# A cached-attention and gated-MLP decode kernel: the first load of each of two queues is issued as two transfers, 16 partitions and then 112

## The chip, the cores and the metric

The kernel runs on one core of a Trainium2 chip. The metric is the device time of one execution in microseconds (us), median of several runs. The core has a matrix engine (PE, TensorE), a vector engine (DVE, VectorE), a scalar engine (ACT), GpSimd (POOL) and SyncE (SP). Data come from the device memory into SBUF, an on-chip memory of 128 partitions, by 16 transfer engines (DMA). In this kernel SP and ACT issue the transfers, each into a queue of its own; the profile calls SP's queue q1 and ACT's q10.

## The reference: what is computed

One token `x` of width 448 goes through two branches, and a gate mixes them.

```python
g = _sigmoid((x * gate_w).sum(-1, keepdims=True))
# A: 16 query heads, 8 K/V heads, 65536 cached positions, head size 256
q = (x @ wq)
scores = einsum("bhqd,bhkd->bhqk", q, k) * (Dh ** -0.5)
a = (softmax(scores) @ v) @ wo
# B: inner width 1792
gate, up = x @ W_gate, x @ W_up
b = (gate * (gate > 0) * up) @ W_down
return g * a + (1 - g) * b
```

The K and V caches are 8 x 65536 x 256 in bf16 each, 268 MB each. All weights together are about 12 MB.

## The kernel before

Every operation and every transfer gets an engine and a key, an intended time. `_Plan` sorts each engine's list by key and puts in the semaphore waits. So the order on each queue is the order of the keys.

K and V come in tiles of 8.39 MB (128 partitions of 65,536 B) into three buffers, `ring0` to `ring2`; a head has four tiles of each. VectorE transposes a K tile in place (L379), PE multiplies it with the spread-out query `xm` (L394, L420), and a row maximum and an exponential follow (L594 to L598). After a head's four K tiles its V tiles are multiplied with the weights. SP issues all the tiles, and waits before each until the buffer is free.

Before the first K tile come the small loads. The plan gives them these places:

- ACT's queue, in this order: the first 384 rows of `W_gate` (L254, semaphore `wf0`, into `wf3[0]`, a part of `ring2`), then `x` (L256), then `gate_w` (L257).
- SP's queue, in this order: the first 384 rows of `wq` (L525, semaphore `wq`, into `wq3`, a part of `ring2`), `W_up` (L540), the last 64 rows of `wq` (L526, into `ring1`), the first K tile (L587, into `ring0`), the last 64 rows of `W_gate` and `W_up` in small pieces (L405, after a memset by POOL), and, once the query's last product is there, `W_down` (L574) and the next K tiles.

For both first loads three rows of the matrix lie side by side in one partition, so a partition takes 3 x 1792 x 2 = 10,752 B of `W_gate` and 3 x 4096 x 2 = 24,576 B of `wq`.

What uses them: `x` starts the chain on VectorE (L310 to L322) that spreads it over partitions; then PE makes the query with `wq` (L345, waits for semaphore `wq`; L352) and the MLP's products with `W_gate` and `W_up` (L550, waits for `wf0`). The first transpose of a K tile comes after them.

The output is 448 values, stored by one transfer (L698) that the program waits for (L706).

Of the kernel before, what the change touches and what calls it, by code (L numbers as in the profile page):

```python
# [24 lines left out]
class _Plan:  # L25
# [13 lines left out]
    def dma(self, eng, key, sem, fn, deps=()):  # L39
        if sem not in self.dsem:  # L40
            self.dsem[sem] = self.es.enter_context(self.nc.semaphore("d_" + sem))
        o = _Op(eng, key, fn, deps, dma=sem)
        self.ops.append(o)
        return o
# [59 lines left out]
def bass_gated_mix__gqa_block_cached__glu_gated_reglu__decode_kernel(  # L104
# [24 lines left out]
    R3 = D // 128  # L129
    NR3 = R3 * 128  # L130
# [13 lines left out]
    with es:  # L144
# [42 lines left out]
        wq3 = ring[2][:, 0:R3 * NQ]  # L187
        wqa = ring[1][:, 0:NQ // 2]
        WB = R3 * NQ
        wf3 = [ring[2][:, WB + i * R3 * F:WB + (i + 1) * R3 * F] for i in range(2)]  # L190
# [18 lines left out]
        op, dma = pl.op, pl.dma  # L209
# [25 lines left out]
        t = 3.0  # L235
# [10 lines left out]
        for kind, i, _ in order:  # L246
# [4 lines left out]
        wo_sb = ring[slot["wo", 0]][:, 0:H * 4 * D].rearrange("p (h s n) -> p h s n", h=H, s=4)  # L251


        d_wg = dma("ac", -10, "wf0", lambda e: e.dma_start(  # L254
            wf3[0], B_W_gate[0:NR3, :].rearrange("(p k) f -> p (k f)", k=R3)))
        d_x = dma("ac", -9, "x", lambda e: e.dma_start(x_row, A_x[0, :, :]))  # L256
        d_gw = dma("ac", -8, "gw", lambda e: e.dma_start(gw_row, gate_w.rearrange("(o d) -> o d", o=1)))  # L257

# [151 lines left out]
        l_, qk, smax, aexp, pv, last = {}, {}, {}, {}, {}, {}  # L410
        pending = []

        def free(key):
            out_ = []
            for f in freed[key]:
                out_.append(l_[f] if isinstance(f, str) else qk[f[1]] if f[0] == "k" else pv[f[1]])
            return out_
# [104 lines left out]

        for kind, i, t in issue:
            if kind == "wq":
                l_["wq"] = dma("sp", t, "wq", lambda e: e.dma_start(wq3, A_wq[0:NR3, :].rearrange("(p k) n -> p (k n)", k=R3)))  # L525
                l_["wqh"] = dma("sp", t + 0.01, "wqh", lambda e: e.dma_start(  # L526
                    wqa, A_wq[NR3:D, :].rearrange("r (c n) -> (r c) n", c=2)))
                tq = tL["wq", 0]
# [9 lines left out]
            elif kind == "gu":  # L538
                t = tL["gu", 0]
# [43 lines left out]
            elif kind == "k":  # L583
                n = i
# [45 lines left out]
            elif kind in ("v", "vp"):  # L630
                if kind == "v":
                    n, lo, hi = i, 0, U
# [12 lines left out]
            elif kind == "wo":  # L645
# [6 lines left out]
                for k, (h0, h1, lo, hi) in enumerate(runs):  # L652
# [3 lines left out]
                    else:  # L656
                        o = wo_sb[:, h0, lo:hi, :]
                        v = A_wo[h0 * 512:h1 * 512, :].rearrange("(p s) n -> p s n", s=4)[:, lo:hi, :]
                    d_ = dma("sp", t + 0.01 * k, "wo%d%d" % (i, k), lambda e, o=o, v=v: e.dma_start(o, v),
                             free(("wo", 0)) if i == 0 else [])  # L660
# [19 lines left out]
        for i in range(len(WOP)):  # L680
            for k, (h, lo, hi) in enumerate(WOP[i]):
                key = tL["wo", i] + 0.01 * k
                if i == 1:
                    key = t7 + (-0.3 if h < NP else 0.6) + 0.01 * k
# [52 lines left out]
```

## Time and profile before

| | us |
|---|---|
| median of 3 runs | 1277.21 (1277.18 to 1277.37) |
| the profiled execution | 1277.21 |
| its span, first to last instruction | 1275.9 |
| VectorE busy | 683.4 (54%) |
| PE busy | 353.7 (28%) |
| ScalarE busy | 56.1 (4%) |
| moved from memory | 549.03 MB |

The span is what the trace covers; 1.31 us of the execution lie around it. The profile's page gives for 40 equal slices of the span the share of time in which each engine was busy and the GB/s that the transfers moved. A group's row gives source line, engine, operation and tiles, then busy time, the mean of one in ns, and the idle time of the engine in front of it with what ended it. The row of an issue gives the size and the time from issue to landing. In the table by stretches each line has the stretch, its length, the busy time of PE, of PE's weight loads, of VectorE, ScalarE and GpSimd, the granted clock of PE, the share of the transfer engines and GB/s. Packets are booked with their bytes where they end, so short stretches swing.

### The profile page before, as it was taken

The page shows a single profiled execution, that of the slowest core. Times are in us where ns is not written, and L with a number is a line of the kernel's source. Part 1 is how long each engine was busy: PE and PEld are TensorE (multiplying, and loading weights), DVE is VectorE, ACT ScalarE, POOL GpSimd, SP SyncE. Part 2 cuts the span into 40 slices and gives each one's busy share as a digit, 9 for nine tenths or more (in the row PEclk, how much of TensorE's full clock was granted, in tenths as well). Part 3 has the DMA queues.
Part 4 walks back from the last instruction along what each step waited for, and adds up shares of the span by engine and source line. Part 5 has one row for each costly group of instructions (what it writes and reads, how often), then busy time and mean ns, then how long its engine had stood idle before and what let it go on. Part 6 is the DMA issues. An engine that isn't in the chain of part 4 may idle for free.

```text
span 1275.9 us, 6860 instructions
## 1 busy us (share of the span) xinstructions
PE 353.7 (28%) x4446; PEld 71.6 (6%) x1875; DVE 683.4 (54%) x271; ACT 56.1 (4%) x104; POOL 10.6 (1%) x23
## 2 busy tenths in 40 slices
PE   3312323313122240133220242211323203322135
PEld 2000000000000000000000000000000000000010
DVE  2688733566534755445555454556535566336521
ACT  0000000000000000000000000000000000000000
POOL 3000000000000000000000000000000000000000
PEclk9566666665666565666755666656666556666577
DMA  9999999999999999999999999999999999999998
GB/s 407 433 436 434 438 428 429 442 427 436 431 426 448 429 428 434 430 434 438 428 434 438 430 434 428 432 438 438 428 428 436 436 438 428 428 438 436 434 417 372
DMA packets 11178, 549.46 MB, mean 431 GB/s; under 512 B 1255, under 2 KB 1386, under 8 KB 2154
## 3 DMA queue, kind: packets, MB, share of 16 engines
q1 hardware_dynamic: 11002, 547.66, 99.3%
q10 hardware_dynamic: 148, 1.38, 0.3%
q8 instruction: 24, 0.39, 0.1%
q14 instruction: 4, 0.03, 0.0%
HBM read 549.03 MB, written 0.00 MB: 430 GB/s over the span
## 4 chain that ended last, share of the span: by engine, by line
DVE 40%; DMA 28%; PE 17%; another core or an unknown queue 12%; ACT 1%; issue 1%; SPq 0%; ACTq 0%; DVEq 0%
DVE ring L379 32%; DMA ring<-in_A_k_cache_dram 24%; PE ST L394 5%; PE ST L420 5%; PE O L420 4%; DMA ring<-in_A_wo_dram 3%; DVE o_sb L429 2%; PE O L488 2%; DVE P L617 1%; DVE P L615 1%; ACT P L598 1%; DMA P<-in_A_x_dram 1%; DVE nmb L596 1%; DVE ST L594 1%
## 5 line engine op out<-in xcount | busy, mean ns | idle before, releaser
L379 DVE STREAM_TRANSPOSE ring<-ring 128x16384 uint32<-128x16384 uint32 (+1 forms) x36 | 552.3, 15345 | 315.9 <-DMA ring<-in_A_k_cache_dram 311.5
L394 PE MATMUL ST<-ring,xm 128*16 128x512 bf16 x1024 | 139.7, 537 | 769.2 <-DVE ring L379 769.2
L420 PE MATMUL ST<-ring,xm 128*16 128x512 bf16 x1024 | 136.7, 526 | 0.0
L420 PE MATMUL O<-ring,P 128*32 128x512 bf16 x1524 | 119.3, 425 | 0.0
L594 DVE COPY_PREDICATED ST<-bm,ST 128x512 f32<-128x512 uint16 x32 | 22.2, 693 | 169.3 <-PE ST L420 169.3
L598 ACT ACTIVATE P<-ST,nmb 128x512 bf16<-128x512 f32 x32 | 45.3, 1415 | 1099.3 <-DVE nmb L596 1099.3
L394 PEld LDWEIGHTS ST<-ring,xm 128*16 128x16 bf16 x1024 | 31.8, 115 | 925.8 <-DVE ring L379 797.9
L488 PE MATMUL O<-ring,P 128*32 128x512 bf16 (+1 forms) x524 | 56.7, 430 | 21.9 <-DMA ring<-in_A_v_cache_dram 21.9
L429 DVE CAST_PREDICATED o_sb<-bm,O 128x512 bf16<-128x512 uint16 (+1 forms) x33 | 22.3, 679 | 62.0 <-PE O L420 58.9
L615 DVE TENSOR_TENSOR P<-P,hs 128x2048 bf16<-128x2048 bf16 x8 | 18.3, 2292 | 8.7 <-ACT hs L612 8.7
L596 DVE TENSOR_REDUCE nmb<-ST 128x1 f32<-128x512 f32 x32 | 22.1, 691 | 1.1
L488 PEld LDWEIGHTS O<-ring,P 128*32 128x32 bf16 (+1 forms) x524 | 15.8, 114 | 119.3 <-issue 92.0
L617 DVE STREAM_TRANSPOSE P<-P 128x2048 bf16<-128x2048 bf16 x8 | 18.5, 2312 | 0.3
L622 PE MATMUL M_ps<-hs,ones_f 128*128 128x2 f32 x16 | 4.7, 363 | 46.0 <-DVE hs L621 46.0
L457 PE MATMUL M_ps<-emat,o_sb 128*64 128x2 bf16 x48 | 3.0, 184 | 22.1 <-ACT o_sb L439 22.1
L598 ACT ACTIVATION_READ_ACCUMULATOR P<-ST,nmb 128x1 f32 x32 | 8.5, 266 | 0.0
L345 PE MATMUL M_ps<-ring,P 128*128 128x256 bf16 x48 | 7.4, 330 | 0.3 <-DVE gb L297 0.3
L310 DVE COPY xm<-P 1x64 bf16<-1x64 bf16 x2 | 0.3, 189 | 11.9 <-DMA P<-in_A_x_dram 11.9
L622 PEld LDWEIGHTS M_ps<-hs,ones_f 128*128 128x128 f32 x16 | 4.0, 311 | 46.7 <-DVE hs L621 46.7
L608 PE MATMUL M_ps<-identf,hs 128*2 128x128 f32 x8 | 2.2, 277 | 15.7 <-DVE hs L606 15.7
L259 POOL MEMSET ring<- 64x7168 bf16 x1 | 6.1, 6064 | 0.3 <-POOLq L722 0.3
L345 PEld LDWEIGHTS M_ps<-ring,P 128*128 128x128 bf16 x48 | 5.6, 118 | 2.0 <-issue 0.4
(96 smaller groups left out, 82.6 us busy)
## 6 DMA issues: line engine op xcount, KB each, us to landing
ring<-in_A_v_cache_dram SPq DMA_DIRECT2D x1, 4096.0 KB, 29.6
ring<-in_A_v_cache_dram SPq DMA_DIRECT2D x2, 2048.0 KB, 36.0
ring<-in_A_wq_dram SPq DMA_DIRECT2D x1, 3072.0 KB, 13.3
ring<-in_A_wo_dram SPq DMA_DIRECT2D x1, 1792.0 KB, 19.4
ring<-in_B_W_down_dram SPq DMA_DIRECT2D x1, 1568.0 KB, 17.2
ring<-in_B_W_gate_dram ACTq DMA_DIRECT2D x1, 1344.0 KB, 13.1
ring<-in_B_W_up_dram SPq DMA_DIRECT2D x1, 1344.0 KB, 15.9
ring<-in_A_wo_dram SPq DMA_DIRECT2D x1, 896.0 KB, 40.0
```

The lines of the kernel that those rows point to most:

```text
L345: ins = e.matmul(QN_ps, xw3[:, kt, 31 - j:159 - j], wq3[:, kt * NQ + j * 256:kt * NQ + (j + 1) * 256], start=(j == 0 and kt == 0), stop=Fa ...
L379: return lambda e: e.transpose(v, v)
L394: ins = e.matmul(o, xm[:, x0:x0 + 16], v, start=st, stop=False, skip_group_check=True, tile_position=(0, 32 * w))
L420: return e.add_instruction(mybir.InstMatmult(name=nc.get_next_instruction_name(), engine=e.engine, ins=[e.lower_ap(v), e.lower_ap(w, for_m ...
L429: return e.copy_predicated(dst, m.to_broadcast(list(src.shape)), src)
L488: ins = e.matmul(o, w, v, start=st, stop=False, skip_group_check=True, tile_position=(0, 32 * g))
L594: join = op("dv", tk + 25.2, lambda e: e.copy_predicated(ST[0][:], bm[:, NB:NB + 1].bitcast(mybir.dt.uint16).to_broadcast([128, 512]), ST[ ...
L596: smax[n] = op("dv", tk + 26, lambda e, n=n, NM=NM, t_=t_: e.tensor_reduce(NM[:, t_:t_ + 1], ST[0][:], AX.X, ALU.max, negate=True), [join, ...
L598: aexp[n] = op("ac", tk + 27, lambda e, n=n, t_=t_, NM=NM, RS=RS, Ph=Ph: e.activation(Ph[:, t_:2048:4], ST[0][:], ACTF.Exp, bias=NM[:, t_: ...
L615: rsc = op("dv", T + 16, lambda e, X=X, pb=pb: e.tensor_tensor(pb, pb, X[:, 12:16].unsqueeze(1).to_broadcast([128, 512, 4]), ALU.mult), [h ...
L617: last["ev", h] = [op("dv", T + 17, lambda e, Ph=Ph: e.transpose(Ph[:], Ph[:]), [rsc])]
L622: l3 = mop("pe", T + 19, lambda e, X=X: e.matmul(LS_ps, ones_f[:, :], X[:, 6:8], start=True, stop=True), [l2, c_one])
```

## The change

Each of the two first loads is issued as two transfers on the same queue, one directly behind the other, by a helper `lead`: partitions 0 to 15, then partitions 16 to 127. Both add to the semaphore that the single transfer had, and what waits for the load waits for both. The keys of the two pieces differ by 0.001, so nothing is issued between them.

```diff
-        d_wg = dma("ac", -10, "wf0", lambda e: e.dma_start(
-            wf3[0], B_W_gate[0:NR3, :].rearrange("(p k) f -> p (k f)", k=R3)))
+        def lead(eng, key, sem, dst, src):
+            for i, (lo, hi) in enumerate(((0, 16), (16, 128))):
+                d_ = dma(eng, key + 0.001 * i, sem, lambda e, lo=lo, hi=hi: e.dma_start(dst[lo:hi, :], src[lo:hi, :]))
+            return d_
+
+        d_wg = lead("ac", -10, "wf0", wf3[0], B_W_gate[0:NR3, :].rearrange("(p k) f -> p (k f)", k=R3))
...
             if kind == "wq":
-                l_["wq"] = dma("sp", t, "wq", lambda e: e.dma_start(wq3, A_wq[0:NR3, :].rearrange("(p k) n -> p (k n)", k=R3)))
+                l_["wq"] = lead("sp", t, "wq", wq3, A_wq[0:NR3, :].rearrange("(p k) n -> p (k n)", k=R3))
```

## The prediction

> **What bounds the kernel now.** I read the slices of the span first, then the queues and the issues, then what the loads' consumers wait for. These are lines of the profile's page.
>
> ```profile
> span 1275.9 us, 6860 instructions
> ...
> DMA  9999999999999999999999999999999999999998
> GB/s 407 433 436 434 438 428 429 442 427 436 431 426 448 429 428 434 430 434 438 428 434 438 430 434 428 432 438 438 428 428 436 436 438 428 428 438 436 434 417 372
> DMA packets 11178, 549.46 MB, mean 431 GB/s; under 512 B 1255, under 2 KB 1386, under 8 KB 2154
> ...
> q1 hardware_dynamic: 11002, 547.66, 99.3%
> q10 hardware_dynamic: 148, 1.38, 0.3%
> ...
> L379 DVE STREAM_TRANSPOSE ring<-ring 128x16384 uint32<-128x16384 uint32 (+1 forms) x36 | 552.3, 15345 | 315.9 <-DMA ring<-in_A_k_cache_dram 311.5
> ...
> ring<-in_A_wq_dram SPq DMA_DIRECT2D x1, 3072.0 KB, 13.3
> ...
> ring<-in_B_W_gate_dram ACTq DMA_DIRECT2D x1, 1344.0 KB, 13.1
> ```
>
> The transfer engines are full in 39 of 40 slices. The two queues (q1 is SP's; q10, with 1.38 MB, is ACT's and holds W_gate) fill 99.6% of the span. VectorE, the busiest compute engine, stands 311.5 us waiting for K tiles. So the bytes set the time. The next view gives the rate by stretches; the last two columns are the transfer engines' share and GB/s.
>
> ```profile
> 0.00:1.60 1.60, 0.00 (x0) 0.00 (x0) 0.70 (x3) 0.00 (x0) 1.07 (x5) 1.00 0.00 0
> 1.60:1.80 0.20, 0.00 (x0) 0.00 (x0) 0.13 (x3) 0.00 (x0) 0.20 (x1) 1.00 1.30 215
> ...
> 2.00:3.50 1.50, 0.00 (x0) 0.00 (x0) 0.07 (x2) 1.28 (x1) 1.50 (x1) 1.00 0.80 298
> 3.50:10.00 6.50, 0.00 (x0) 0.00 (x0) 0.00 (x0) 0.00 (x0) 5.75 (x11) 1.00 1.02 435
> ...
> 100.00:1220.00 1120.00, 297.31 (x3806) 53.40 (x1502) 616.64 (x204) 51.11 (x96) 0.00 (x0) 0.62 1.00 433
> ...
> 1273.60:1275.90 2.30, 0.55 (x8) 0.26 (x8) 0.38 (x1) 0.34 (x1) 0.00 (x0) 1.00 0.00 0
> ```
>
> No byte moves for about 1.6 us. Then 435 GB/s are reached while weights come, and 433 GB/s hold for 1,120 us of K and V. In the last 2.3 us only the result's 0.9 KB moves. The kernel is 1.6 us of silence, one unbroken transfer, and a tail. A delay inside the transfer can be taken up only where the queue has gaps. The issues say that it has none: a K tile lands 50.3 us and a V tile 34.9 us after its issue.
>
> ```profile
> ring<-in_A_k_cache_dram SPq DMA_DIRECT2D x32, 50.3
> ring<-in_A_v_cache_dram SPq DMA_DIRECT2D x31, 34.9
> ```
>
> A tile is 128 x 65,536 B = 8.39 MB, which is 19.4 us at 433 GB/s, so at its issue one or two tiles still stand ahead of it. What is lost in the first 15 us therefore arrives at the end in full.
>
> **The change part by part.** W_gate (ACT's first issue, L254) and wq (SP's first, L525) become two transfers each, partitions 0 to 15 and then 16 to 127. Bytes, destinations and every other instruction's order stay; PE, VectorE and GpSimd run the same list. Both pieces count on the same semaphore, and the consumers wait for both. Four terms follow: the issue, the completion, the start, and where the rows are written.
>
> *Issue.* The timeline of the issues:
>
> ```profile
> 0.73 0.40 ACTq L254 DMA_DIRECT2D ring<-in_B_W_gate_dram  x1
> ...
> 0.74 0.40 SPq L525 DMA_DIRECT2D ring<-in_A_wq_dram  x1
> ...
> 1.20 0.43 SPq L540 DMA_DIRECT2D ring<-in_B_W_up_dram  x1
> ...
> 2.15 0.48 SPq L587 DMA_DIRECT2D ring<-in_A_k_cache_dram  x1
> 6.82 3.01 SPq L405 DMA_DIRECT2D ring<-in_B_W_gate_dram  x4
> ```
>
> One more issue on each queue costs 0.40 to 0.48 us of sequencer time. Behind it on ACT stand x, gate_w and an activation at 16.73 us that needs them; behind it on SP stand W_up, the rest of wq and the first K tile, and then L405, which is held until 6.82 us anyway. W_gate and wq together are 1.38 + 3.15 = 4.52 MB, 10.4 us at 435 GB/s, so what is issued 0.45 us later still joins a queue that is busy until about 12 us. I take 0; without that cover it would be 0.45 us.
>
> *Completion.* Each extra transfer adds one small completion packet per transfer engine. The run already has 1255 packets under 512 B, some 78 per engine, and holds 433 GB/s with them. Two more per engine: 0.
>
> *Start.* This is the only place for a gain. The first issue ends at 1.13 us and bytes appear at 1.6 to 1.8 us. If a list an eighth as long let them flow at once, 0.5 us would be won. The ramp adds what 2.00 to 3.50 us falls short of: (435 - 298) / 435 x 1.5 = 0.47 us, if it vanished. So the bounds are -1.0 and 0. The nearest row is the last one-row store, which waits 0.8 us for its landing after its issue:
>
> ```profile
> SPq L706 <- DMA out_dram<-P: 0.8, 1, 0.8
> ```
>
> One row needs as long as that, so most of the silence has nothing to do with the count of rows. I take -0.2 us.
>
> [...]
>
> *Where the rows are written.* One row is W_gate's 10,752 B or wq's 24,576 B. At 435 / 16 = 27.2 GB/s per engine they take 0.395 and 0.904 us, 1.30 us together. Before, both transfers spread over all 128 partitions. After, each engine's first piece of each queue is one row (16 rows, 16 engines), and these 16 rows lie in neighbouring partitions. The rate is 435 GB/s for short weight rows and 433 for 64 KB rows: a fixed path sets it, not the memory or the length of rows. Nothing here tells whether that path belongs to the engine or to the partitions written. If it belongs to the engine, this term is 0. If 16 equal paths serve 128 partitions, eight each, then 16 neighbouring partitions have between two paths (eights lie together) and 16 (dealt one by one). With two, every lead row takes eight times as long: 7 x 1.30 = 9.1 us more. With four, it takes four times: 3 x 1.30 = 3.9 us. With 16 it is 0. I take four paths, the middle step between the ends, so **+3.9 us**.
>
> No later work wins this back: every engine carries one row of each lead, and its remaining bytes are as many as before. For the remaining 112 rows, seven per engine, the bounds are 0 (each engine on a path of its own) and seven more such quadrupled rounds, 7 x 3.9 = 27.3 us (the 16 engines always on 16 neighbouring rows). If each engine has seven rows in a block, most are on different paths and only some rounds meet in pairs. I take one round doubled, **+1.3 us**, because a block per engine is the nearest to the full-rate rows of before.
>
> [...]
>
> **The sum.** 0 + 0 - 0.2 + 3.9 + 1.3 = +5.0 us on the profiled execution's own 1277.21 us (span 1275.9 and 1.31 around it), which is also the median of the runs: **1282.2 us**. The wait that becomes later is x's, which stands behind W_gate on ACT's queue and holds VectorE, and after it the q chain, until SP issues again:
>
> ```profile
> 1.16 12.82 DMA P<-in_A_x_dram
> ...
> 27.86 0.36 SPq L574
> ...
> 28.27 36.15 DMA ring<-in_A_k_cache_dram
> ```
>
> ```profile
> 37.70 8.71 DVE L379 STREAM_TRANSPOSE ring<-ring 128x8192 uint32<-128x8192 uint32 x1 [7.13 <-DMA ring<-in_A_k_cache_dram]
> ```
>
> At 28.27 us the first K tile, which is transposed from 37.70 us, is still coming, so that chain has some 9 us in hand. Both ends move by the same 5 us. The delay goes through the bytes, not through the chain.
>
> **The rivals.** *The engine owns the path* (not slower). Then the spread of rows costs nothing and only the start term is left: -0.2, between -1.0 and 0, so 1277.0 us. For it: the full rate is the same whatever is loaded, and the DMA share is 1.00 with 16 engines. Against it: all the large transfers of this run cover all 128 partitions, so the rate was never seen with fewer. It decides if the first K tile lands no later than now.
>
> *Faster by over 0.2%.* It would have to win 2.55 us. All the silence is 1.6 us and the ramp 0.5 us, and at least the issue's 0.40 us stays; the bound of -1.0 excludes it as far as the rows go.
>
> *All eight rounds are bunched.* If the 112 rows are dealt to the 16 engines in turn, every round sits on 16 neighbouring rows: 8 x 3.9 = 31.3 us, 1308 us. For it: nothing in the rows tells how 112 rows are dealt. Against it: with 128 rows in the same loads the rate is full, so the dealing then does not bunch.
>
> *A mild form.* Only some engines meet, or the leads slip past one another, and +0.5 to +2.5 us remain, about 1278.7 us. The queues' interleaving speaks for it; against it stands that every engine must take its row.
>
> **How the numbers follow.** The forecast (shared paths, +2.55 to +9.8 us: 1279.8 to 1287) gets 0.56. That all long stretches run at one rate, whatever the row, marks a fixed path, and no row here has the full rate with few partitions. The engine-owned path gets 0.27, the mild form 0.10, all rounds bunched 0.05, faster by over 0.2% 0.02. The bound of 0.2% is 2.55 us, about what a measurement of this kernel can tell from no change. Slower is 0.56 + 0.05 = 0.61, same 0.27 + 0.10 = 0.37, faster 0.02. The range reaches from the engine-owned case, 1276.6, to the shared paths' upper end, 1287: it leaves out the bunched rounds, the faster case, and edges of the rest, under 0.2. The forecast's own range is 1279.8 to 1287.
>
> **What would show it.** In the rate by stretches, 2 to 8 us must fall well below 435 GB/s, for a while towards a quarter; x and the first K tile must land 4 to 6 us later (the first transpose near 42.7 us instead of 37.70); from then on tiles must come at the old rate, 433 GB/s, and the end move by the same amount. It is the engine-owned path if 3.50 to 10.00 us still shows 435 GB/s and the first transpose stays within 1 us. The start term is right if bytes still first appear at 1.4 to 1.8 us. The forecast is wrong in its cover, not its cause, if the first K tile is late and the end is not.

## The result: 10.2 us slower, lost before the first K tile

| | before | after |
|---|---|---|
| median, us | 1277.34 (6 runs, 1277.18 to 1277.58) | 1287.58 (6 runs, 1286.80 to 1287.95) |
| profiled execution, us | 1277.21 | 1287.26 |
| its span, us | 1275.9 | 1286.0 |

The ratio is 1.0079, with a 95% interval of 1.0069 to 1.0090: +10.24 us. The forecast was +5.0. Lines of the page of the changed kernel:

```profile
span 1286.0 us, 6863 instructions
...
GB/s 294 416 444 427 435 439 426 435 430 435 428 443 431 426 445 428 429 431 442 427 432 441 425 434 437 430 429 440 431 431 439 432 426 435 437 428 441 431 418 367
DMA packets 11210, 549.46 MB, mean 427 GB/s; under 512 B 1287, under 2 KB 1418, under 8 KB 2186
...
q1 hardware_dynamic: 11018, 547.66, 99.1%
q10 hardware_dynamic: 164, 1.38, 0.5%
```

The bytes are the same. There are 32 more packets under 512 B, one per extra transfer and engine. The first slice fell from 407 to 294 GB/s; over a slice of 32 us that is 3.6 MB that came later. The second fell from 433 to 416, 0.5 MB more; the two together are some 9.5 us at 433 GB/s. The other slices scatter as before. The rate by stretches of the changed kernel (last two columns: share of the transfer engines, GB/s):

```profile
0.00:1.60 1.60, 0.00 (x0) 0.00 (x0) 0.70 (x3) 0.00 (x0) 1.07 (x5) 1.00 0.00 0
1.60:1.80 0.20, 0.00 (x0) 0.00 (x0) 0.14 (x3) 0.00 (x0) 0.20 (x1) 1.00 3.57 614
...
2.00:3.50 1.50, 0.00 (x0) 0.00 (x0) 0.07 (x2) 1.00 (x1) 1.50 (x1) 1.00 0.32 49
3.50:10.00 6.50, 0.00 (x0) 0.00 (x0) 0.00 (x0) 0.29 (x1) 5.75 (x11) 1.00 0.97 174
10.00:20.00 10.00, 0.00 (x0) 0.00 (x0) 0.00 (x0) 0.00 (x0) 1.93 (x8) 1.00 1.05 270
20.00:100.00 80.00, 28.06 (x288) 12.59 (x212) 53.10 (x45) 1.97 (x4) 0.00 (x0) 0.70 1.01 429
100.00:1220.00 1120.00, 297.77 (x3803) 53.09 (x1499) 617.56 (x197) 50.69 (x94) 0.00 (x0) 0.62 1.00 433
```

These stretches book a row, its bytes and its time, where it starts, not where it ends as was said above; hence a share of 3.57 in 0.2 us. The silence at the start is no shorter: the first row starts at 1.75 us, before at 1.76. From 3.5 to 10 us the engines are as busy as before (0.97 against 1.02) but move 174 GB/s instead of 435: a packet takes longer, no engine is idle. In this view the narrow writes show as a full share at a low rate. The rate stays low until the last of the split rows is written, at 23.1 us:

```profile
18.00:22.00 4.00, 0.00 (x0) 0.00 (x0) 0.00 (x0) 0.00 (x0) 0.00 (x0) 1.00 0.92 215
```

After that all is as it was. The sizes in the table of issues tell the pieces apart (KB, us from issue to landing):

```profile
ring<-in_A_wq_dram SPq DMA_DIRECT2D x1, 2688.0 KB, 22.9
...
ring<-in_B_W_gate_dram ACTq DMA_DIRECT2D x1, 1176.0 KB, 23.1
...
ring<-in_A_wq_dram SPq DMA_DIRECT2D x1, 384.0 KB, 7.0
...
ring<-in_B_W_gate_dram ACTq DMA_DIRECT2D x1, 168.0 KB, 7.2
```

The two leads, 0.565 MB together, need 7 us to land, and the remainders 23 us, where the whole loads had landed after 13.3 and 13.1 us. The timeline shows what the first users see:

```profile
24.02 0.29 DVE L314 COPY xm<-P 1x64 bf16<-1x64 bf16 x2 [21.92 <-DMA P<-in_A_x_dram]
...
47.96 8.71 DVE L383 STREAM_TRANSPOSE ring<-ring 128x8192 uint32<-128x8192 uint32 x1 [6.63 <-DMA ring<-in_A_k_cache_dram]
```

The first transpose starts at 47.96 instead of 37.70 us, 10.3 us later, and the span is 10.1 us longer. All of the loss is there before the first K tile, and none is won back or added in the following 1,238 us.

The trace also holds the time of every row's own transfer; a row of W_gate is known by its 10,752 B, one of wq by its 24,576 B. Medians, in us:

| rows | W_gate | wq |
|---|---|---|
| before, without each engine's first | 0.404 | 0.912 |
| changed, the 16 lead rows | 1.607 | 2.389 |
| changed, the 112 rows behind them | 0.726 | 1.608 |

The lead rows of W_gate took 4.0 times as long as a row before, those of wq 2.6 times; why these not more is open. And of the 112 rows behind them not one ran at the old rate: the shortest took 0.427 and 0.967 us.

### The profile page after: what moved, and what is told of

It is laid out like the page before. It is cut to its first block, busy times and chain, and to the rows that moved or that the text cites. A ratio compares the mean times of both kernels' runs of the same rounds, so it can differ in the third digit from the quotient of the medians.

```text
span 1286.0 us, 6863 instructions
## 1 busy us (share of the span) xinstructions
PE 355.9 (28%) x4447; PEld 72.0 (6%) x1875; DVE 683.5 (53%) x271; ACT 56.1 (4%) x104; POOL 10.7 (1%) x23
## 4 chain that ended last, share of the span: by engine, by line
DVE 40%; DMA 29%; PE 17%; another core or an unknown queue 12%; ACT 1%; issue 1%; SPq 0%; ACTq 0%; DVEq 0%
DVE ring L383 32%; DMA ring<-in_A_k_cache_dram 24%; PE ST L398 5%; PE ST L424 5%; PE O L424 4%; DMA ring<-in_A_wo_dram 3%; DMA P<-in_A_x_dram 2%; DVE o_sb L433 2%; PE O L492 2%; DVE P L621 1%; DVE P L619 1%; ACT P L602 1%; DVE nmb L600 1%; DVE ST L598 1%; PE M_ps L349 1%
## 5 line engine op out<-in xcount | busy, mean ns | idle before, releaser
L398 PE MATMUL ST<-ring,xm 128*16 128x512 bf16 x1024 | 141.9, 546 | 766.4 <-DVE ring L383 766.4
L424 PE MATMUL ST<-ring,xm 128*16 128x512 bf16 x1024 | 138.8, 534 | 0.0
L612 PE MATMUL M_ps<-identf,hs 128*2 128x128 f32 x8 | 2.2, 277 | 15.8 <-DVE hs L610 15.8
## 6 DMA issues: line engine op xcount, KB each, us to landing
ring<-in_B_W_down_dram SPq DMA_DIRECT2D x1, 1568.0 KB, 15.8
ring<-in_B_W_gate_dram ACTq DMA_DIRECT2D x1, 1176.0 KB, 23.1
```

Of the source, the lines that this page charges most:

```text
L398: ins = e.matmul(o, xm[:, x0:x0 + 16], v, start=st, stop=False, skip_group_check=True, tile_position=(0, 32 * w))
L424: return e.add_instruction(mybir.InstMatmult(name=nc.get_next_instruction_name(), engine=e.engine, ins=[e.lower_ap(v), e.lower_ap(w, for_m ...
```

## The experiments

Theory A is the forecast's: partitions in groups share a path for writing, so the rate depends on which partitions are written at the same time. The rivals are that an extra or a short transfer costs something by itself (B, C), that the reading side is slow (D), and that a slow first transfer delays the start (E). Differences are against the kernel before on the same chip (1277.28, 1277.45 and 1277.50 us in the three series).

### Is it the number of transfers? Split along the row

```diff
-            for i, (lo, hi) in enumerate(((0, 16), (16, 128))):
-                ... dst[lo:hi, :], src[lo:hi, :]
+            n = dst.shape[1]
+            for i, (lo, hi) in enumerate(((0, n // 8), (n // 8, n))):
+                ... dst[:, lo:hi], src[:, lo:hi]
```

> Both loads are still split in two, an eighth ahead, but along the row: all 128 partitions get the first eighth of their row, then all get the rest. Theory A (writes into neighbouring partitions share a path, so a transfer needs all 128 partitions for the full rate): the loss is gone, the time is within 0.5 us of the kernel before, 1276.8 to 1277.8; 435 GB/s from 3.5 to 10 us; first K tile transposed near 37.7 us. Theory B (a second transfer on each queue, or a short first one, costs by itself about 5 us): about +10 us, 1287, as in the changed kernel.

Measured: 1277.56 us (11 runs), ratio 1.0002 (0.9993 to 1.0011). Its rate by stretches and its first transpose:

```profile
1.60:1.80 0.20, 0.00 (x0) 0.00 (x0) 0.13 (x3) 0.00 (x0) 0.20 (x1) 1.00 0.04 13
...
3.50:10.00 6.50, 0.00 (x0) 0.00 (x0) 0.00 (x0) 0.27 (x1) 5.76 (x11) 1.00 1.05 444
```

```profile
38.10 8.71 DVE L384 STREAM_TRANSPOSE ring<-ring 128x8192 uint32<-128x8192 uint32 x1 [7.98 <-DMA ring<-in_A_k_cache_dram]
```

As many transfers, the same lead of an eighth, and no loss (+0.3 us): theory B falls. Nor is there a gain; the smaller first transfer brings no byte sooner (the first starts at 1.76 us, as before).

### One load at a time

W_gate split, wq whole; and the reverse.

```diff
-                l_["wq"] = lead("sp", t, "wq", wq3, ...)
+                l_["wq"] = whole("sp", t, "wq", wq3, ...)
```

> Only W_gate (ACT's queue) is split at partition 16; wq is one transfer. Theory A: the loss goes by bytes that are written in narrow transfers; W_gate has 10,752 of the 35,328 B of a partition, 30% of 10.2 us: +2 to +4 us, 1279.3 to 1281.3. Theory B (so much per additional transfer): half of it, +5 us, 1282.4.

> Only wq (SP's queue) is split at partition 16; W_gate is one transfer. Theory A: 70% of the bytes, +6 to +8.5 us, 1283.3 to 1285.8. Theory B: half of the loss, +5 us, 1282.4; e2 and e3 alike.

Measured: 1281.99 us (+4.7, 1280.75 to 1282.40 in 5 runs) and 1284.35 us (+7.1). The larger load cost more, and wq is inside theory A's bounds. W_gate is above them, and the two add up to 11.8, not 10.2 us. So the loss isn't simply shared by bytes. The trace shows a part of the reason: with W_gate alone split, the rows of the whole wq were held up too, 1.264 us each in place of 0.912. Which rows of the two queues meet on which path, these runs do not show.

### Halves

```diff
-            for i, (lo, hi) in enumerate(((0, 16), (16, 128))):
+            for i, (lo, hi) in enumerate(((0, 64), (64, 128))):
```

> Both loads split at partition 64 instead of 16. Theory A, with paths that belong to groups of four neighbours and repeat every 32 partitions: each half reaches half of the paths, every row takes twice as long, 8 rounds x 1.3 us = +10.4 us, 1287 to 1288, spread evenly over the load (about 217 GB/s from 2 to 20 us). Theory A with eight neighbours to a path gives the same. Theory C (only the 16-row lead or the odd count of 112 rows is slow): nothing, 1277 to 1278.

Measured: 1287.47 us (+10.2). The rate by stretches:

```profile
3.50:10.00 6.50, 0.00 (x0) 0.00 (x0) 0.00 (x0) 0.81 (x1) 5.76 (x11) 1.00 1.11 239
10.00:20.00 10.00, 0.00 (x0) 0.00 (x0) 0.00 (x0) 0.00 (x0) 1.94 (x8) 1.00 0.97 209
```

With neither a short lead nor an odd count of rows, both halves ran at about half of 435 GB/s (239 and 209 in these stretches). The time is nearly that of the changed kernel, but that likeness says nothing about the changed kernel's cause: theory A gives this one 8 rounds x 1.3 us, and the changed kernel another sum.

### Sixteen rows each: every fourth, every second, neighbours

These four kernels make the same six transfers per load (four of 16 rows in partitions 32 to 95, then 0 to 31 and 96 to 127) and differ only in which rows go together. In all four, SP issues W_up ahead of wq's last piece. Two or three runs were made of each; the two of "every second" lie 2.05 us apart (1287.83 and 1289.88).

```diff
-            for i, (lo, hi) in enumerate(((0, 16), (16, 128))):
+            for i, (o, v) in enumerate(((slice(32, 93, 4), slice(32, 93, 4)), (slice(33, 94, 4), slice(33, 94, 4)),
+                                        ..., (slice(0, 32), slice(0, 32)), (slice(96, 128), slice(96, 128)))):   # apart
+            ... (slice(32, 48), slice(32, 48)), (slice(48, 64), slice(48, 64)), ...                              # near
+            ... (slice(32, 48), slice(32, 93, 4)), (slice(48, 64), slice(33, 94, 4)), ...                        # near from apart
+            ... (slice(32, 63, 2), slice(32, 63, 2)), (slice(33, 64, 2), slice(33, 64, 2)), ...                  # step 2
```

> Both loads in six transfers: four of 16 rows each, taking every fourth partition of 32 to 95 (32, 36, ... 92; 33, 37, ...), then partitions 0 to 31, then 96 to 127. Theory A (paths belong to groups of four neighbouring partitions, 0 to 3 with 32 to 35, and so on, with 64 to 127 on other paths): the four transfers of 16 rows put each engine on a path of its own and run at the full rate; the two of 32 rows reach half of the paths and take twice as long, 4 rounds x 1.3 us = +5.3 us, 1282.6. Theory C (a transfer of 16 rows is slow as such): +5.3 and 4 rounds x 3.9 us = +21 us, 1298.

> As e5_apart, with the same six sizes in the same order, but the four transfers of 16 rows take neighbouring partitions: 32 to 47, 48 to 63, 64 to 79, 80 to 95. Theory A: four engines to a path in each, 4 rounds x 3 x 1.3 us = 15.8 us above e5_apart, 1298. Theory C: as e5_apart.

> Destinations as in e6_near (16 neighbouring partitions), sources as in e5_apart (every fourth row block of memory); W_gate and wq then stand in another order, and the output is another. Theory A (the path is on the writing side): as e6_near, 1298. Theory D (16 neighbouring rows of the memory are slow to read): as e5_apart, 1282.6.

> As e5_apart, but the four transfers of 16 rows take every second partition: 32, 34, ... 62; 33, ...; 64, 66, ... 94; 65, .... Theory A with groups of four neighbours: two engines to a path, 4 rounds x 1.3 us above e5_apart, 1287.9. With groups of two neighbours it would be as e5_apart; with groups of eight as e6_near.

| rows written together | us | against before | against "apart" |
|---|---|---|---|
| every fourth | 1284.46 | +7.0 | |
| every second | 1288.85 | +11.4 | +4.4 (expected 5.3) |
| neighbours | 1298.51 | +21.1 | +14.1 (expected 15.8) |
| neighbours, read from every fourth | 1297.47 | +20.0 | +13.0 (expected 15.8) |

The rate from 5 to 10 us, in this order of kernels:

```profile
5.00:10.00 5.00, 0.00 (x0) 0.00 (x0) 0.00 (x0) 1.28 (x1) 4.26 (x11) 1.00 1.05 344
```

```profile
5.00:10.00 5.00, 0.00 (x0) 0.00 (x0) 0.00 (x0) 1.28 (x1) 4.24 (x11) 1.00 1.08 226
```

```profile
5.00:10.00 5.00, 0.00 (x0) 0.00 (x0) 0.00 (x0) 0.79 (x1) 4.24 (x11) 1.00 0.99 113
```

```profile
5.00:10.00 5.00, 0.00 (x0) 0.00 (x0) 0.00 (x0) 0.81 (x1) 4.26 (x11) 1.00 1.06 125
```

The first of these rates holds a part of the slow 32-row pieces. The single rows of the 16-row pieces tell it cleanly (medians in us, without each engine's first):

| rows written together | W_gate | wq |
|---|---|---|
| all 128 (the kernel before) | 0.404 | 0.912 |
| every fourth | 0.404 | 0.919 |
| every second | 0.840 | 1.893 |
| neighbours | 1.597 | 3.328 |

A transfer of 16 rows isn't slow as such, so theory C falls: the same transfers cost 14 us or nothing like it, by their partitions alone. Neighbours ran at about a quarter of the rate of a full load (1.597 us for a row of W_gate against 0.404), every second partition at about half (0.840), every fourth at all of it (0.404). So in partitions 32 to 95, where these transfers lie, four neighbours were written as if they shared one path. By theory A's reckoning, groups of two neighbours would have given the neighbours half the rate and every second all of it; groups of eight, an eighth and a quarter. Which groups outside 32 to 95 share a path with which, as the expectation of "every fourth" has it (0 to 3 with 32 to 35), no run here shows; the halves fit it (209 to 239 GB/s). Where the rows are read from made 1 us of the 14 (13.0 against 14.1): the slow side is the writing, and theory D falls. The 1.7 us by which "apart" exceeds its expectation are not explained; its first row starts 0.4 us later than before (2.13 against 1.76 us), which could be a part.

### Order, and the 112 rows alone

```diff
-            for i, (lo, hi) in enumerate(((0, 16), (16, 128))):
+            for i, (lo, hi) in enumerate(((0, 112), (112, 128))):    # lead last
```

```diff
-            for i, (lo, hi) in enumerate(((0, 16), (16, 128))):
-                ...
+            blank.append(op("dv", -0.29, lambda e: e.memset(dst[0:16, :], 0.0)))      # rest alone
+            return dma(eng, key, sem, lambda e: e.dma_start(dst[16:128, :], src[16:128, :]))
```

```diff
+            ... (slice(0, 16), slice(0, 16)), (slice(16, 122, 7), slice(16, 122, 7)), (slice(17, 123, 7), ...), ...   # step 7
```

> The same two sizes in the other order: partitions 0 to 111, then 112 to 127. Theory A: the loss belongs to which rows go together, not to what comes first: +10 us, 1286.5 to 1288.5. Theory E (a slow first transfer delays the start): most of the loss goes, since the short transfer is no longer first; 1277 to 1281.

> Only the transfers of partitions 16 to 127 are made; partitions 0 to 15 of both loads are set to zero by VectorE instead, so an eighth of W_gate's and wq's rows is left out. 0.565 MB less is 1.3 us less at the full rate. If the 112 rows lose the 1.3 us that the prediction gave them: 1277.4 - 1.3 + 1.3 = 1277.4. If the lead costs 3.9 us and the 112 rows have the rest of the 10.2 us, 6.3 us: 1282.4. If they lose nothing and the lead all of it: 1276.1.

> Partitions 0 to 15, and then the 112 rows as seven transfers of 16 rows, each with every seventh partition (16, 23, ... 121; 17, 24, ...). If the single transfer of 112 rows gives each engine a block of seven rows, this is the same work in the same order: as the changed kernel, 1287 to 1288. If it deals the rows to the engines in turn, the changed kernel would have cost over 30 us already, and this one need not match it. If six more transfers on each queue cost anything by themselves, it is above 1288.

Lead last: 1288.30 us, +10.8. The loss does not go away when the short transfer comes last; theory E falls.

The 112 rows alone: 1282.62 us, +5.1 although 1.3 us of bytes are missing. So the transfers of 112 rows lose 5.1 + 1.3 = 6.4 us, and by difference the leads have the rest of the changed kernel's 10.2, 3.8 us. The rate while these rows alone are written:

```profile
5.00:10.00 5.00, 0.00 (x0) 0.00 (x0) 4.72 (x1) 0.00 (x0) 4.26 (x11) 1.00 0.94 281
```

The first transpose of this kernel, with no lead at all, is 5.3 us later than before:

```profile
42.96 8.71 DVE L384 STREAM_TRANSPOSE ring<-ring 128x8192 uint32<-128x8192 uint32 x1 [6.70 <-DMA ring<-in_A_k_cache_dram]
```

Step 7: 1287.82 us, the changed kernel's 1287.58 within the scatter. If each of these transfers gives its 16 rows to the engines in order, the seven give one engine rows 16, 17, ... 22, the next one 23 to 29, and so on, and they cost as much as the single one of 112 rows. That fits blocks of seven rows per engine; it does not prove them, since another dealing could cost as much, and since the order on the queue is not quite the same: SP issues W_up at 4.02 us, ahead of wq's last three transfers. Six more transfers on each queue cost nothing visible (1287.82 against 1287.58 us).

No version here is faster than the kernel before.

## Why the prediction was right in kind and too small

**What bounds the kernel.** Right. 433 GB/s hold from 100 to 1,220 us in both kernels; 10.3 us lost by the first transpose are 10.1 us in the span. The q chain stayed covered: its restart of the loads (27.86 us before, 38.60 after) moved with the K tile and still comes 9 us ahead of the first transpose.

**Issue and completion, 0.** Right: step 7 has eight transfers per load instead of two and costs the same (1287.82 against 1287.58 us).

**Start, -0.2 us.** Too hopeful. Bytes first appear in 1.60 to 1.80 us as before, and the split along the row, which keeps only this term, has a ratio of 1.0002. It is 0, the bound that was given.

**The lead rows, +3.9 us.** Right in kind: of the three cases the middle one (four engines to a path) is the one that the ladder of every fourth, every second and neighbouring rows fits (0.404, 0.840 and 1.597 us for a row of W_gate), measured in partitions 32 to 95. Its size is less sure. By difference between two kernels it is 3.8 us. In the changed kernel's own records an engine's two lead rows took 4.0 us on average, where its first two rows took 1.9 us before: 2.1 us more. That the 3.8 is so near to 3.9 is partly luck.

**The remaining 112 rows, +1.3 us.** This is the step that failed, the term that was mis-sized: "I take one round doubled". It measured 6.4 us. The 112 rows of both loads are 3.96 MB, 9.1 us at 435 GB/s; with 6.4 more they took 15.5, or 255 GB/s on average, 1.7 times as long. So it is not one round of seven that is doubled: the extra time is that of about five doubled rounds, and the records spread it over all seven. In the changed kernel itself the 14 rows that an engine carries behind its leads took 16.3 us instead of 9.2, so there the term is 7.1 us. The argument "a block per engine is the nearest to the full-rate rows of before" took that dealing for harmless. That the rows were slowed is measured (medians of 0.726 us in place of 0.404 for W_gate and 1.608 in place of 0.912 for wq); whether each engine has a block of them, and which of them met, is open.

**The sum.** 0 + 0 + 0 + 3.8 + 6.4 = 10.2 us; it closes because the 3.8 is a difference. The upper end of the range, 1287.0, was drawn 0.6 us too low for the same reason: it had room for a heavier lead or for a dearer remainder, but not for the remainder at five times its estimate. Neither end of the range came from the terms: the prediction shows no working for the +9.8, and at the lower end its bound of -1.0 gives 1276.2, not 1276.6.

**The rivals.** "The engine owns the path" is out: with sixteen rows to a transfer in each case, the engines ran at about a quarter of their rate onto neighbouring partitions (1.597 us for a row of W_gate) and at all of it onto every fourth (0.404). The bunched rounds (1308) did not occur with 112 rows; the neighbours' kernel shows what they look like, for half of the rows. The mild form, +0.5 to +2.5 us, falls by the measured 10.2.

## What to carry to other kernels

A load in a stream that is bound by transfers should write all 128 partitions in one transfer, as the two loads did before, at 435 GB/s. If it has to be split, split it along the row, which cost nothing here (1277.56 against 1277.28 us), and not over ranges of neighbouring partitions, which here halved or quartered the rate for as long as the pieces lasted (209 to 239 GB/s for halves, 113 for 16 neighbours). When a share of the transfer engines stays near 1.0 while GB/s fall (here 0.97 at 174 GB/s), look at which partitions are written together. When the stream has no gaps, a loss of the first 25 us is still there, whole, a millisecond later (10.3 us at the first transpose, 10.1 in the span); and when a transfer is cut in two, price the long remainder as carefully as the short lead.

## What was not expected of the hardware

The two transfers of 112 partitions ran at about 255 GB/s, although they cover seven eighths of the partitions; the two of 128 ran at 435. Sixteen rows placed four partitions apart from 32 on were written as fast as rows of a full load (0.404 us for a row of W_gate), 16 neighbours four times slower (1.597 us). A split load slowed an unsplit one on the other queue (1.264 instead of 0.912 us for a row of wq). And a lead of an eighth did not bring the first byte sooner, neither narrow nor wide (1.75 and 1.76 us, before 1.76).
